# Weight preparation of an attention and SiLU network block on one NeuronCore: raw buffers, engine split and the order of the first loads

## The chip, the cores and the metric

The kernel runs on one core of a Trainium2 chip. The metric is device time in microseconds (us) of one execution. Five engines run side by side, each through its own instruction queue in order: TensorE (PE, matrix products and transposes; PEld is its weight load), VectorE (DVE), ScalarE (ACT), GpSimd (POOL) and SyncE (SP, which here only issues DMAs). Instructions wait for one another through semaphores.

## The reference

Eight batches of 576 tokens, eight heads of 64. Attention keeps only scores within `tau` of the row's maximum; its output, 4608 tokens of 512 features, goes through a two-layer network with 2048 hidden units.

```python
scores = scale * np.matmul(q, k.transpose(0, 1, 3, 2))
thresh = np.max(scores, axis=-1, keepdims=True) - tau
scores = np.where(scores >= thresh, scores, -1000000000.0)
scores = scores - np.max(scores, axis=-1, keepdims=True)
attn = np.exp(scores)
attn = attn / (np.sum(attn, axis=-1, keepdims=True) + 1e-09)
attn_out = np.matmul(attn, v)
...
h = x @ w_in
g = h * (1.0 / (1.0 + np.exp(-h)))
return g @ w_out
```

q, k and v are float32; w_in and w_out are float64 and reach the kernel as their raw words, so it decodes them itself.

## The kernel before, in words

**Tiles of attention.** The rows of the score matrices are cut into tiles of 128 query rows by 576 keys, one after the other. Batch 0 has 16 "low" tiles (tokens 0 to 255 of all heads; here called tiles 0 to 15), then 20 "high" ones (tiles 16 to 35); batch 1 has 16 and 20 as well (36 to 71); each later batch has 36. A tile passes through PE scores (`scores`, L452 in batch 0 in full float32, L464 later with split operands), DVE row maximum (L474), ACT exponential (L484), DVE mask and row sum (L493, with the small L477, L497 and L501), a scaling by the reciprocal row sum (POOL L507 in batch 0, ACT L511 later), and a transpose: in batch 0 on PE (L403, L408) with ACT copies out of PSUM (L416, L417), later by POOL splits into two float16 parts (L519, L522, L525) and a DMA transpose. Then `av_direct` (L426) or `av` (L550) multiplies by v, and `av_post` (L568, L569) writes the features x as two float16 parts. Only one PSUM bank holds an `a` product.

**The network.** For each half of a batch there are 16 h-units (L593: 12 products each, then ACT tanh L601, DVE L602, ACT L608, DVE L609, which leave the hidden layer in `gbuf` as two float16 parts) and 16 o-units (L624: 12 products each, four to an output block, ACT copy L634, store). The f-th h-unit needs four of the 16 blocks of w_in; every o-unit needs four blocks of w_out.

**The weights.** Each matrix is 16 blocks of 128 x 512. `load_weights` (L180) brings 512 KB of raw words to a buffer: half of the w_in blocks go to places in `gbuf` that the hidden layer doesn't use yet, the other half of w_in and all of w_out to a pool `wraw` with two buffers. `decode_weights` turns the words into float32 (ACT L190, DVE L193 and L196) and adds the block's Gram product to a PSUM bank (PE L208), from whose maximum (L213) `pow2_scales` forms one power-of-two scale for the matrix (L110 to L150). `split_weights` makes two float16 parts of each block: w_in by POOL (L225, scaling in place), ACT (L228) and POOL (L229, subtraction), w_out by ACT (L220) and DVE (L221).

**What sets the order.** The program is recorded in steps of one tile; `at(t, f)` puts work at step t, `W_PLAN` spreads loads, decodes, scale and splits of the two matrices over steps, and `pri` raises the priority of what it wraps. A scheduler then orders each engine's queue by priority and by a timeline that it keeps; on the chip the queues run in that order. `load_v` and `vmax` of batch 0 are at steps -4 and 0, where `vscale` follows at step 1.

Of the kernel before, what the change touches and what calls it, by code (L numbers as in the profile page):

```python
# [15 lines left out]
ALU = mybir.AluOpType  # L16
AX = mybir.AxisListType
# [18 lines left out]

W_PLAN = ((0, 0, 10, 13, 0), (16, 9, 22, 36, 0))
PRI_S, PRI_SOFT1, PRI_SOFT2 = 1600, 50, 200
# [13 lines left out]
def attention_moe(  # L52
# [52 lines left out]
    def pow2_scales(mx, name, own=None, squared=False):  # L105
# [6 lines left out]
        nc.scalar.activation(diag, ident, AF.Copy, scale=one)  # L112
        allp = bank([P, P], f"{name}_ps", own)
        nc.tensor.matmul(allp, ones, diag, start=True, stop=True)
# [53 lines left out]
    def load_weights(i):  # L168
        if i < 4 * NK and i % 8 < 4:
            o = 1024 * (i % 8)  # L170
            t = gbuf.bitcast(I32)[:, o : o + 1024].rearrange("p (c w) -> p c w", w=2)
        else:
            t = stage.tile([P, 512, 2], I32, tag="wraw", name=f"wraw_{i}", bufs=2)
        if i < 4 * NK:
            n, c = divmod(i, NK)
            src = w_words[0][c * P : (c + 1) * P, 1024 * n : 1024 * (n + 1)]
        else:
            f = i - 4 * NK
            src = w_words[1][f * P : (f + 1) * P, :]
        nc.sync.dma_start(out=t.rearrange("p c w -> p (c w)"), in_=src)  # L180
        wraw[i] = t

    def decode_weights(i):


        t = wraw.pop(i)
        low, top = t[:, :, 0], t[:, :, 1]
        w = wst[:, i + WSPARE, :]
        wbits = w.bitcast(I32)
        nc.scalar.activation(  # L190
            w, top.bitcast(F32), AF.Prelu, scale=2.0**-112, alpha=2.0**32
        )
        nc.vector.tensor_scalar(  # L193
            out=wbits, in0=wbits, scalar1=3, scalar2=None, op0=ALU.logical_shift_left
        )
        nc.vector.scalar_tensor_tensor(  # L196
            out=wbits, in0=low, scalar=29, in1=wbits,
            op0=ALU.logical_shift_right, op1=ALU.bitwise_or,
        )


        n, c = divmod(i, 4)
        if c == 0:
            wps[n] = bank([P, P], f"wps_{n}", 2)
        upper = w.bitcast(BF16).rearrange("p (c t) -> p c t", t=2)[:, :, 1]
        for j in range(4):
            part = upper[:, j * P : (j + 1) * P]
            nc.tensor.matmul(  # L208
                wps[n], part, part,
                start=(c == 0 and j == 0), stop=(c == 3 and j == 3),  # L210
            )
        if c == 3:
            nc.vector.tensor_reduce(out=wmx[:, n : n + 1], in_=wps[n], op=ALU.max, axis=AX.X)  # L213

    def split_weights(i):
        w = wst[:, i + WSPARE, :]
        hi = w16[:, i, 0:512]
        sc = wsc["in" if i < 4 * NK else "out"][:, 0:1]
        if i >= 4 * NK:
            nc.scalar.activation(hi, w, AF.Copy, scale=sc)  # L220
# [3 lines left out]
            return  # L224
        nc.gpsimd.tensor_scalar(  # L225
            out=w, in0=w, scalar1=sc, scalar2=1.0, op0=ALU.mult, op1=ALU.mult
        )
        nc.scalar.activation(hi, w, AF.Copy)  # L228
# [488 lines left out]
    for b in range(B):  # L717
        u = start[b, 0]
        for p in range(NPAIR):
            if b == 0:  # L720
                at(-4, lambda p=p: load_v(0, p))
                at(0, lambda p=p: vmax(0, p))
            elif b == 1:
# [3 lines left out]
            else:  # L727
# [3 lines left out]
                at(u + pace * p + pace // 2, lambda b=b, p=p: split_v(b, p))  # L731
        at((1, u + 2)[b] if b < 2 else u - 2, lambda b=b: vscale(b))

# [15 lines left out]
    for first, t0, t1, t2, hp in W_PLAN:  # L749
# [5 lines left out]
        for i in range(16):  # L755
            at(t1 + i * (t2 - t1) // 16, pri(hp, lambda i=i + first: split_weights(i)))
    at(W_PLAN[0][3], lambda: batch_scales_in(0))
# [23 lines left out]

    scores(0)
    t = 0
# [93 lines left out]
```

## Time and profile before

| what | value |
|---|---|
| median of 3 runs | 1230.53 us (1227.3 to 1231.17) |
| profiled execution | 1225.66 us, of which the span of its instructions is 1223.9 us |
| busy: PE, DVE, ACT, POOL | 1150.3, 933.7, 796.4, 707.5 us |
| granted PE clock, mean | 0.987 |
| chain that ended last | PE 63%, DVE 11%, DMA 10%, POOL 7% of the span |

The profile is of one execution. "Busy" is the time in which an engine has an instruction in work; for PE the ends are modelled. Idle time of an engine is given with what released the next instruction. "x40" is a count of instructions, and a float32 product counts as two.

### The profile page before, as it was taken

How to read it: one execution, taken by the hardware profiler on the slowest of the kernel's cores; microseconds unless marked ns; L12 is line 12 of the kernel's file. 1: busy time of each engine (PE TensorE's matmuls, PEld its weight loads, DVE VectorE, ACT ScalarE, POOL GpSimd, SP SyncE). 2: the span in 40 equal slices, each digit the busy share in tenths (PEclk: the TensorE clock that was granted, in tenths of full speed). 3: DMA queues.
4: the chain of work that ended last, by engine and by line, in shares of the span. 5: the costliest groups of instructions: out<-in, count | busy, mean ns of one | idle time of the engine just before them, and what ended most of it. 6: DMA issues, size and time to landing. Idle time of an engine off the chain costs nothing.

```text
span 1223.9 us, 27062 instructions
## 1 busy us (share of the span) xinstructions
PE 1150.3 (94%) x9474; PEld 899.2 (73%) x9474; DVE 933.7 (76%) x2625; ACT 796.4 (65%) x1505; POOL 707.5 (58%) x902
## 2 busy tenths in 40 slices
PE   6868799999899799999999999999999999999998
PEld 4545567777786577787777777788778877777777
DVE  7988988988999988889889858886788858333330
ACT  6667875876867777777777747785677756333331
POOL 2385357887877587886888428781778547100000
PEclk9979999999999999999999999999999999999999
DMA  9553148889788777886987448772877356200000
GB/s 309 185 161 95 41 108 173 160 160 177 132 177 141 160 137 139 150 165 151 167 149 145 114 94 155 146 136 82 153 150 142 77 92 116 42 11 16 16 10 25
DMA packets 340887, 151.73 MB, mean 124 GB/s; under 512 B 305936, under 2 KB 317200, under 8 KB 340752
## 3 DMA queue, kind: packets, MB, share of 16 engines
q1 hardware_dynamic: 340752, 150.01, 59.1%
q8 instruction: 75, 1.23, 0.4%
q14 instruction: 60, 0.49, 0.1%
HBM read 66.19 MB, written 9.44 MB: 62 GB/s over the span
## 4 chain that ended last, share of the span: by engine, by line
PE 63%; DVE 11%; DMA 10%; POOL 7%; issue 4%; ACT 4%; SPq 1%; POOLq 0%; ACTq 0%; DVEq 0%
PE o L624 24%; PE h L593 21%; PE s L464 9%; PE a L550 7%; DMA wT<-hl 4%; POOL hl L522 3%; DMA wraw<-in_w_out 3%; DVE w L493 2%; POOL hl L519 2%; DVE sm L474 2%; DVE qstack L350 2%; POOL hl L525 1%; DMA wraw<-in_w_in 1%; ACT w L484 1%; ACT w L511 1%
## 5 line engine op out<-in xcount | busy, mean ns | idle before, releaser
L593 PE MATMUL h<-x,wst 128*128 128x288 f16 (+2 forms) x3072 | 425.8, 288 | 7.8 <-DVE gbuf L609 5.0
L624 PE MATMUL o<-gbuf,wst 128*128 128x288 f16 (+2 forms) x3072 | 417.9, 286 | 2.4 <-ACT wst L634 2.4
L593 PEld LDWEIGHTS <-wst 128*128 128x128 f16 x3072 | 292.2, 98 | 95.7 <-issue 16.9
L624 PEld LDWEIGHTS <-wst 128*128 128x128 f16 x3072 | 292.7, 98 | 83.7 <-issue 7.4
L522 POOL TENSOR_TENSOR hl<-w,hl 128x512 f16<-128x512 f32 x252 | 302.6, 1201 | 12.8
L519 POOL TENSOR_SCALAR hl<-w 128x576 f16<-128x576 f32 x252 | 172.2, 686 | 193.4 <-ACT w L511 115.7
L484 ACT ACTIVATE w<-s,sm 128x576 f32<-128x576 f32 x288 | 211.6, 739 | 91.9 <-DVE sm L474 39.1
L493 DVE SCALAR_TENSOR_TENSOR w<-s,sm,w 128x576 f32<-128x576 f32 x288 | 232.0, 812 | 39.9 <-ACT w L484 37.8
L474 DVE TENSOR_REDUCE sm<-s 128x1 f32<-128x576 f32 x288 | 214.4, 749 | 28.7 <-PE s L464 21.8
L511 ACT ACTIVATE w<-w,sm 128x576 f32<-128x576 f32 x252 | 191.4, 771 | 52.1 <-DVE sm L501 50.1
L602 DVE SCALAR_TENSOR_TENSOR h<-th,h 128x288 f32<-128x288 f32 (+2 forms) x256 | 116.2, 455 | 113.7 <-ACT th L601 112.3
L601 ACT ACTIVATE th<-h,msc 128x288 f32<-128x288 f32 (+2 forms) x256 | 126.6, 498 | 103.2 <-PE h L593 101.8
L464 PE MATMUL s<-khi,qstack 128*128 128x288 f32 x560 | 144.3, 338 | 12.7 <-DVE w L493 9.9
L608 ACT ACTIVATE gbuf<-h 128x288 f16<-128x288 f32 (+2 forms) x256 | 104.3, 408 | 78.2 <-DVE h L602 77.5
L609 DVE SCALAR_TENSOR_TENSOR gbuf<-h,gbuf 128x288 f16<-128x288 f32 (+2 forms) x256 | 115.3, 452 | 41.9 <-ACT gbuf L608 41.0
L550 PE MATMUL a<-wT,v 128*64 128x288 f16 (+2 forms) x1568 | 115.0, 289 | 10.8 <-DMA wT<-hl 10.6
L360 POOL TENSOR_TENSOR klo<-kraw,khi 128x576 fp32r<-128x576 f32 x64 | 94.5, 1476 | 47.1 <-ACT khi L358 47.0
L464 PE MATMUL s<-klo,qstack 128*128 128x288 f32 x560 | 120.8, 296 | 0.0
L464 PEld LDWEIGHTS s<-khi,qstack 128*128 128x128 f32 x560 | 87.7, 190 | 31.9 <-issue 15.4
L550 PEld LDWEIGHTS <-v 128*64 128x64 f16 x1568 | 84.5, 110 | 33.7 <-issue 22.1
L464 PEld LDWEIGHTS s<-klo,qstack 128*128 128x128 f32 x560 | 90.4, 189 | 0.6
L525 POOL TENSOR_TENSOR hl<-w,hl 128x64 f16<-128x64 f32 x252 | 89.5, 355 | 0.0
(101 smaller groups left out, 930.4 us busy)
## 6 DMA issues: line engine op xcount, KB each, us to landing
kraw<-in_kT SPq DMA_DIRECT2D x128, 144.0 KB, 3.0
qraw<-in_qT SPq DMA_DIRECT2D x96, 144.0 KB, 3.0
vraw<-in_vL SPq DMA_DIRECT2D x32, 320.0 KB, 3.6
wraw<-in_w_out SPq DMA_DIRECT2D x16, 512.0 KB, 3.7
out_t<-wst SPq DMA_DIRECT2D x48, 144.0 KB, 2.1
wT<-hl SPq DMA_TRANSPOSE x280, 3.4
gbuf<-in_w_in SPq DMA_DIRECT2D x8, 512.0 KB, 6.2
wraw<-in_w_in SPq DMA_DIRECT2D x8, 512.0 KB, 5.1
```

What stands on the lines that cost most here:

```text
L464: nc.tensor.matmul(s_ps[:, j, :HALF], lhs, kk[:, j * HALF : (j + 1) * HALF], start=(n == 0), stop=(n == len(seq) - 1),)
L474: nc.vector.tensor_reduce(out=negm, in_=s_ps[:, :, :HALF], op=ALU.max, axis=AX.XY, negate=True)
L484: nc.scalar.activation(wtile[t].rearrange("p (j c) -> p j c", j=2), sps[t][:, :, :HALF], AF.Exp, bias=small[t][:, 0:1],)
L493: nc.vector.scalar_tensor_tensor(out=w3, in0=s_ps[:, :, :HALF], scalar=sm[:, 1:2], in1=w3, op0=ALU.is_ge, op1=ALU.mult, accum_out=sm[:, 2:3],)
L511: nc.scalar.activation(w, w, AF.Copy, scale=r)
L519: nc.gpsimd.tensor_scalar(out=fl[:, 0:S], in0=w, scalar1=1.0, scalar2=1.0, op0=ALU.mult, op1=ALU.mult)
L522: nc.gpsimd.tensor_tensor(out=fl[:, 640:1152], in0=w[:, 0:512], in1=fl[:, 0:512], op=ALU.subtract)
L550: nc.tensor.matmul(a_ps[odd * D : (odd + 1) * D, :n], vt[:, lo_v, odd, kv, :], wT[v, b * H + 2 * p + odd][:, kw, c0 - base : c0 - base + n ...
L593: nc.tensor.matmul(ph[:, :n], wi(c, f, lo_w), x16[b, lo_x][:, c, c0 : c0 + n], start=(k == 0), stop=(k == 11),)
L601: nc.scalar.activation(th[:, :n], ph[:, :n], AF.Tanh, scale=moe_sc[b][:, 0:1])
L602: nc.vector.scalar_tensor_tensor(out=ph[:, :n], in0=th[:, :n], scalar=1.0, in1=ph[:, :n], op0=ALU.add, op1=ALU.mult,)
L624: nc.tensor.matmul(ps[:, :n], wo(f, d, lo_w), g[:, lo_g, :n], start=(f == 0 and k == 0), stop=(f == NF - 1 and k == 2),)
```

## The change

Five things change.

- The raw-word buffers: besides the w_in blocks that already lie in `gbuf`, every block whose number leaves 2 or 3 when divided by 4 now goes to one of two further places there (6400 and 7424), so `wraw` with its two buffers holds only the other blocks.
- The second parts: odd blocks of w_in are split by ACT and one DVE instruction, even ones stay with POOL, ACT, POOL. Blocks of w_out are scaled in place by a DVE instruction (new), copied by ACT, and subtracted by POOL.
- Loads, decodes and scale of w_out get priority 150; no split gets a raised one. The splits of w_out are spread to step 38, from 36.
- v of batch 0 is loaded at step -1, its maximum is at step 2 and its scale at step 3. The first `scores` gets a raised priority.
- The product with which the scale of w_out is spread over partitions writes into the second half of the last Gram bank, instead of a bank taken anew.

```diff
-W_PLAN = ((0, 0, 10, 13, 0), (16, 9, 22, 36, 0))
+W_PLAN = ((0, 0, 10, 13, 0), (16, 9, 22, 38, 150))
...
-        allp = bank([P, P], f"{name}_ps", own)
+        allp = wps[7][:, P : 2 * P] if name == "o_w" else bank([P, P], f"{name}_ps", own)
...
     def load_weights(i):
         if i < 4 * NK and i % 8 < 4:
             o = 1024 * (i % 8)
+        else:
+            o = (None, None, 6400, 7424)[i % 4]
+        if o is not None:
             t = gbuf.bitcast(I32)[:, o : o + 1024].rearrange("p (c w) -> p c w", w=2)
         else:
             t = stage.tile([P, 512, 2], I32, tag="wraw", name=f"wraw_{i}", bufs=2)
...
     def split_weights(i):
-        if i >= 4 * NK:
+        if i < 4 * NK and i % 2:
             nc.scalar.activation(hi, w, AF.Copy, scale=sc)
             nc.vector.scalar_tensor_tensor(
                 out=w16[:, i, 512:1024], in0=w, scalar=sc, in1=hi, op0=ALU.mult, op1=ALU.subtract
             )
             return
-        nc.gpsimd.tensor_scalar(
-            out=w, in0=w, scalar1=sc, scalar2=1.0, op0=ALU.mult, op1=ALU.mult
-        )
+        if i < 4 * NK:
+            nc.gpsimd.tensor_scalar(
+                out=w, in0=w, scalar1=sc, scalar2=1.0, op0=ALU.mult, op1=ALU.mult
+            )
+        else:
+            nc.vector.tensor_scalar(out=w, in0=w, scalar1=sc, scalar2=None, op0=ALU.mult)
         nc.scalar.activation(hi, w, AF.Copy)
         nc.gpsimd.tensor_tensor(
             out=w16[:, i, 512:1024], in0=w, in1=hi, op=ALU.subtract
...
-                at(-4, lambda p=p: load_v(0, p))
-                at(0, lambda p=p: vmax(0, p))
+                at(-1, lambda p=p: load_v(0, p))
+                at(2, lambda p=p: vmax(0, p))
...
-            at(t1 + i * (t2 - t1) // 16, pri(hp, lambda i=i + first: split_weights(i)))
+            at(t1 + i * (t2 - t1) // 16, pri(0, lambda i=i + first: split_weights(i)))
...
-    scores(0)
+    pri(2 * PRI_S, lambda: scores(0))()
```

The scheduler's order moves with it, on all engines, over the first half of the program. Three places follow. The first is the start of DVE's queue, `sm` being a tile's small column, `s` its scores, `w_0` its exponentials, `wst` the decoded weights, `v`-names the scale of v. Before:

```order
L390 TENSOR_SCALAR gbuf<-gbuf,gate 64x256 x2
L474 TENSOR_REDUCE sm_132<-s_129 128x1
L474 TENSOR_REDUCE sm_183<-s_136 128x1
L477 TENSOR_SCALAR sm_132<-sm_132,ntau 128x1
L268 TENSOR_REDUCE vmx_161<-vps_140 128x1
L477 TENSOR_SCALAR sm_183<-sm_183,ntau 128x1
L493 SCALAR_TENSOR_TENSOR w_0_133,sm_132<-s_129,sm_132,w_0_133 128x576
L110 TENSOR_REDUCE v_one<-vmx_161 128x1
L193 TENSOR_SCALAR wst<-wst 128x512
```

And in the changed kernel (its lines are 6 higher from there on, L196 is the old L193 and L199 the old L196):

```order
L396 TENSOR_SCALAR gbuf<-gbuf,gate 64x256 x2
L480 TENSOR_REDUCE sm_132<-s_129 128x1
L196 TENSOR_SCALAR wst<-wst 128x512
L483 TENSOR_SCALAR sm_132<-sm_132,ntau 128x1
L199 SCALAR_TENSOR_TENSOR wst<-gbuf,wst 128x512
L499 SCALAR_TENSOR_TENSOR w_0_133,sm_132<-s_129,sm_132,w_0_133 128x576
L480 TENSOR_REDUCE sm_160<-s_136 128x1
```

The first decode moved ahead of the first mask, and the maximum of v far back.

The second is POOL's queue where the splits of w_in begin; `w_13` and so on are exponentials that wait for their scaling. Before:

```order
L507 TENSOR_SCALAR w_13_754<-w_13_754,sm_753 128x576
L225 TENSOR_SCALAR wst<-wst,i_w_sc 128x512 x16
L229 TENSOR_TENSOR wst<-wst 128x512 x2
L507 TENSOR_SCALAR w_14_795<-w_14_795,sm_794 128x576
L507 TENSOR_SCALAR w_15_839<-w_15_839,sm_838 128x576
L507 TENSOR_SCALAR w_28_1137<-w_28_1137,sm_1136 128x576
```

And now:

```order
L513 TENSOR_SCALAR w_14_779<-w_14_779,sm_778 128x576
L229 TENSOR_SCALAR wst<-wst,i_w_sc 128x512 x8
L235 TENSOR_TENSOR wst<-wst 128x512 x2
L513 TENSOR_SCALAR w_15_823<-w_15_823,sm_822 128x576
L513 TENSOR_SCALAR w_28_1120<-w_28_1120,sm_1119 128x576
L235 TENSOR_TENSOR wst<-wst 128x512 x2
```

The block of scalings between two tiles is half as long, and stands one tile later.

The third is PE's queue where the first o-unit (`o_0_0`) begins; `a_3_256` is the last product of batch 0 with v, `s` with `khi` a score of batch 1, `h_0_15` the last h-unit of the first half. Before:

```order
L426 MATMUL a_3_256_2038<-wT_6_1787,vraw_3_117 64x320
L426 MATMUL a_3_256_2038<-wT_7_1880,vraw_3_117 64x320
L464 MATMUL s_2151<-khi_2013,qstack_85 128x288 x2
L464 MATMUL s_2151<-klo_2015,qstack_85 128x288 x2
L624 LDWEIGHTS wst
L624 MATMUL o_0_0_1535<-gbuf,wst 128x256
```

And now:

```order
L599 MATMUL h_0_15_1490<-x_0_1_443,wst 128x256
L599 LDWEIGHTS wst
L599 MATMUL h_0_15_1490<-x_0_0_442,wst 128x256
L630 LDWEIGHTS wst
L630 MATMUL o_0_0_1529<-gbuf,wst 128x256
```

Before, the o-units begin behind the scores of tile 41 and the end of batch 0's attention; now they begin behind the scores of tile 33, with tiles 34 and 35 of batch 0 still to come.

More of the change, by code (lines that the diff above doesn't have):

```diff
@@ L203, in decode_weights @@
         if c == 0:
-            wps[n] = bank([P, P], f"wps_{n}", 2)
+            wps[n] = bank([P, 2 * P if n == 7 else P], f"wps_{n}", 2)
         upper = w.bitcast(BF16).rearrange("p (c t) -> p c t", t=2)[:, :, 1]
@@ L208, in decode_weights @@
             nc.tensor.matmul(
-                wps[n], part, part,
+                wps[n][:, 0:P], part, part,
                 start=(c == 0 and j == 0), stop=(c == 3 and j == 3),
@@ L212, in decode_weights @@
         if c == 3:
-            nc.vector.tensor_reduce(out=wmx[:, n : n + 1], in_=wps[n], op=ALU.max, axis=AX.X)
+            nc.vector.tensor_reduce(out=wmx[:, n : n + 1], in_=wps[n][:, 0:P], op=ALU.max, axis=AX.X)
     def split_weights(i):
@@ L731, in attention_moe @@
                 at(u + pace * p + pace // 2, lambda b=b, p=p: split_v(b, p))
-        at((1, u + 2)[b] if b < 2 else u - 2, lambda b=b: vscale(b))
+        at((3, u + 2)[b] if b < 2 else u - 2, lambda b=b: vscale(b))
     def pri(offset, f):
```

## The prediction

> **What bounds the kernel now.** I read the busy times by stretch first, then groups by line, then the timeline at the ends of stages.
>
> ```profile
> core 0: us, PE busy (x) PEld busy (x) DVE busy (x) ACT busy (x) POOL busy (x), PEclk, DMA share, GB/s
> 0.00:60.00 60.00, 45.66 (x282) 30.25 (x283) 50.64 (x163) 38.03 (x74) 15.31 (x28) 0.97 0.76 247
> 60.00:75.40 15.40, 8.76 (x42) 4.59 (x40) 12.41 (x33) 9.12 (x18) 15.38 (x19) 0.92 0.52 157
> 75.40:111.00 35.60, 27.11 (x152) 18.30 (x153) 30.05 (x68) 26.56 (x55) 26.89 (x25) 0.80 0.48 150
> 111.00:178.00 67.00, 57.51 (x385) 40.81 (x385) 57.58 (x170) 49.73 (x111) 23.05 (x25) 0.95 0.20 52
> 178.00:210.30 32.30, 31.16 (x292) 26.83 (x291) 27.36 (x65) 19.29 (x35) 24.56 (x28) 1.00 0.82 185
> 210.30:253.70 43.40, 39.19 (x325) 29.48 (x324) 41.52 (x120) 37.26 (x72) 36.60 (x46) 1.00 0.83 157
> 253.70:450.00 196.30, 179.70 (x1518) 141.28 (x1516) 177.15 (x492) 142.85 (x257) 151.99 (x195) 0.99 0.81 156
> 450.00:1050.00 600.00, 590.66 (x5089) 471.82 (x5086) 489.76 (x1416) 419.60 (x768) 413.75 (x539) 1.00 0.70 133
> ```
>
> From 450 us on PE is busy 98% of the time: nothing there is to be had. PE's idle time lies ahead: 29.5 us to 111, 9.5 to 178, 1.1, 4.2, then 16.6 to 450. To 111 us DVE has most work (93.1 us); 60 to 75.4 belongs to POOL.
>
> The stages end with the last maximum of a w_out block (A, 111), the last product for the first 16 h-units' results (B, 178), 16 o-units (C, 210.3, where PE's next h-unit starts) and 16 more h-units (D, 253.7):
>
> ```profile
> 110.82 0.27 DVE L213 TENSOR_REDUCE wmx<-wps 128x1 f32<-128x128 f32 x1
> 177.42 0.41 DVE L609 SCALAR_TENSOR_TENSOR gbuf<-h,gbuf 128x256 f16<-128x256 f32 x1
> 210.09 0.57 PE L593 MATMUL h<-x,wst 128*128 128x320 f16 x3
> 251.73 1.93 PE L593 MATMUL h<-x,wst 128*128 128x320 f16 x13
> ```
>
> **Stage A: what goes and what comes.** The start, and the POOL block:
>
> ```profile
> 2.87 2.01 SPq L250 DMA_DIRECT2D vraw<-in_vL  x4
> 8.73 1.42 DVE L474 TENSOR_REDUCE sm<-s 128x1 f32<-128x576 f32 x2 [3.15 <-PE s L452]
> 11.12 0.66 ACT L190 ACTIVATE wst<-gbuf 128x512 f32<-128x512 f32 x1 [0.85 <-DMA gbuf<-in_w_in]
> 60.02 12.72 POOL L225 TENSOR_SCALAR wst<-wst,i_w_sc 128x512 f32<-128x512 f32 x16 [2.51 <-DVE i_w_sc L145]
> 75.39 3.67 POOL L507 TENSOR_SCALAR w<-w,sm 128x576 f32<-128x576 f32 x4
> ```
>
> Before, tile 0's second score product stands behind tile 1's, and the four loads of v ahead of w_in. Undone, the first maximum comes one tile's two products sooner, 3.15 of idle shrinking by some 1.8 us (between 0 and 3.15). The four v loads, passed on SP's queue by two w_in blocks, then delay blocks 2 and 3 instead; v itself is not needed before tile 1 is transposed. Net: 1.8. From 60 to 75.4 no L507 runs, so no tile is transposed; now eight scalings and two subtractions stand there.
>
> ```profile
> L193 DVE TENSOR_SCALAR wst<-wst x32: 404/426/1281, 11.8 to 108.1; 128x512 int32<-128x512 int32 x32
> L196 DVE SCALAR_TENSOR_TENSOR wst<-wraw,wst 128x512 int32<-128x512 int32 x24 | 20.2, 842 | 0.1
> L196 DVE SCALAR_TENSOR_TENSOR wst<-gbuf,wst 128x512 int32<-128x512 int32 x8 | 5.4, 680 | 0.0
> L193 DVE TENSOR_SCALAR wst<-wst 128x512 int32<-128x512 int32 x32 | 17.8, 557 | 7.5 <-ACT wst L190 7.5
> L190 ACT ACTIVATE wst<-wraw 128x512 f32<-128x512 f32 x15 | 10.1, 675 | 12.0 <-DMA wraw<-in_w_out 12.0
> L493 DVE SCALAR_TENSOR_TENSOR w<-s,sm,w 128x576 f32<-128x576 f32 x25 | 20.0, 807 | 1.5 <-ACT w L484 1.3
> L474 DVE TENSOR_REDUCE sm<-s 128x1 f32<-128x576 f32 x26 | 19.2, 746 | 4.0 <-PE s L452 4.0
> L477 DVE TENSOR_SCALAR sm<-sm,ntau 128x1 f32<-128x1 f32 x26 | 5.2, 203 | 0.1
> L501 DVE RECIPROCAL sm<-sm 128x1 f32<-128x1 f32 x24 | 3.7, 153 | 0.1
> L221 DVE SCALAR_TENSOR_TENSOR wst<-wst,o_w_sc x16: 726/743/1485, 124.6 to 150.3; 128x512 f16<-128x512 f32 x16
> L229 POOL TENSOR_TENSOR wst<-wst x16: 1147/1326/1611, 72.7 to 105.2; 128x512 f16<-128x512 f32 x16
> ```
>
> ACT waited 12.0 us for w_out's raw blocks, which wait for two buffers; that made 7.5 us of idle on DVE. With four buffers I take half of it away. In the changed program, seven tiles fewer stand on DVE ahead of the last decode (19 maxima for 26, 17 masks for 24), because w_out's decode has priority: 7 x (0.746 + 0.807 + 0.203 + 2 x 0.153) = 14.4 us; with one x part and two h parts gone (some 1.3 us) and two L221 kinds come (1.5), 14.2. L193 and L196 took 17.8 - 32 x 0.426 = 4.2 and 20.2 - 24 x 0.68 = 3.9 us over their undisturbed times, nearly all while POOL worked; POOL's work on w_in now lies later and is half, so I take 4 off. A: 93.1 - 14.2 - 4 = 75 busy, and of 17.9 idle 1.8 and 3.75 go: **87 us** instead of 111 (76 with no idle but the start's and no disturbance, 97 with all of both).
>
> **Stage B.** Counted in the order, DVE loses against before: ten L221 kinds (7.4), two masks, two splits of q, a v maximum, one scale, about 5 us; and gets 16 scalings of w_out. No row shows float32 scaling on DVE at this size; L193 has its shape with one input: 0.43 to 1.28. I take 0.43: 6.9. So 57.6 - 12.4 + 6.9 = 52. On PE:
>
> ```profile
> L452 PE MATMUL s<-kd,gbuf 128*128 128x288 f32 x40 | 11.9, 423 | 2.7 <-DVE w L493 2.7
> L403 PE MATMUL tm<-ident,w 128*128 128x128 f32 x52 | 8.4, 286 | 3.8 <-ACT wT L416 3.7
> L408 PE MATMUL tl<-ident,w 128*128 128x128 f32 x13 | 3.8, 289 | 0.9 <-ACT wT L417 0.9
> L593 PE MATMUL h<-x,wst 128*128 128x256 f16 x168 | 22.8, 291 | 2.5 <-DVE gbuf L609 2.5
> L464 PE MATMUL s<-khi,qstack 128*128 128x288 f32 x20 | 5.1, 337 | 0.7 <-DVE w L493 0.7
> L464 PE MATMUL s<-klo,qstack 128*128 128x288 f32 x20 | 4.3, 294 | 0.0
> L550 PE MATMUL a<-wT,v 128*64 128x256 f16 x56 | 3.7, 275 | 0.4 <-DMA wT<-hl 0.4
> ```
>
> A tile of batch 0 costs 1.19 us of scores (four rows of 40) and 0.94 of transposes, one of batch 1 0.94 of scores (ten tiles). B now holds all 16 h-units (2 more, 3.3 us) and 15 scores of batch 0 instead of 10 with 4 of batch 1 (2.2): 63 us. Before, 9.5 were idle; with DVE lighter I take 6: **69** (63 to 73). POOL's 16 subtractions of w_out (16 x 1.33 = 21 us) lie beside this: it was busy 23 of 67. B ends at 156, not 178: 22 us ahead.
>
> But less is done there: six tiles' scores (6.2), seven tiles' transposes (6.6), half an `a` pair (1.6) are owed on PE, 14.4 us; on DVE about 21 (seven maxima, nine masks and what goes with them). So 22 us of lead are **7.6** if PE bounds what follows, 1 if DVE does.
>
> **C and D.** C keeps its o-units, swaps 11 scores of batch 1 (10.3), two `a` products (56 rows, 3.7) and part of an h-unit (1.2) for 6 scores (6.2) and 7 transposes (6.2, some rows run ahead): 3 us less on PE, 29. It ends at 185 instead of 210.3; PE now owes 17.4. DVE has only six tiles there instead of 11, and owes 21 + 5 x 2.06 = 31. D gets five tiles more: DVE 41.5 + 5 x 2.06 + some 2 of splits = 54, above PE's 48; with 1.9 idle as before, 56. D ends at 241, 12.7 ahead, and PE owes six scores and one `a` product, 5.6 + 1.9 = 7.5: a gain of 5. By the 64th h-unit, near 430, it owes five scores and two products, 8.4. **Gain: about 4.** Further on both orders come together, on a stretch where PE is never idle for long, so I let the 4 stand.
>
> The sum is against the profiled execution: 1223.9 - 4 = 1219.9 of span, with 1.8 around it 1221.7 where it had 1225.66. That one is 4.9 below the median; on the median of 1230.53 it is 1226.5.
>
> **Edits at nothing.** ACT swaps eight L220 for eight L228 of about the same length, beside PE's bound in B. The new places in `gbuf` are read out by the decode in A, long before the hidden layer's second half gets there in D; were they not, its h parts would wait. The scale's product in the last Gram bank saves a wait for a bank that the h-units use, and is at most one unit, 22.8 / 14 = 1.6 us, inside B's 63 to 73. A later end of w_out's splits (step 38) is covered by the h-units in front of the first o-unit; bare, it would cost one POOL subtraction, 1.3 us.
>
> [...] The mean L193 is 0.56 us with a longest of 1.28, so POOL does cost DVE time. [...]
>
> **The rivals.**
>
> *The scalings wait (slower).* The 16 scalings of w_out stand nearly in one burst on DVE, between the second and third h-unit's parts. Masks and h parts are queued behind them, the two h banks are full, and PE waits. At the longest L193, 1.28, they take 20.5 instead of 6.9, 13.6 more: 1226.5 + 13.6 = 1240. From 0.43 + 4/16 = 0.68 each on the gain is gone. For it: the disturbed L193; against: half of them ran at 0.426. Chance 0.12.
>
> *What is owed is paid on DVE (slower).* In C DVE is idle half the time. If the stages to 450, where it was busy 90%, must make up all of the 31 us, the lead of 25 is spent and 6 more: 1236. It decides from D at 60 us on, where the lead (253.7 - 185 - 60 = 8.7) is about what PE owes. For it: the row to 450; against: PE has 16.6 us idle there too. Chance 0.13.
>
> [...] If the tiles' pipeline no longer stops, A ends at 80 and B holds 66: 10 more, 1216. For it: PE's granted clock of 0.80 behind the stop; against: DVE is 84% busy. Chance 0.20.
>
> *No gain.* If buffers weren't it, DMAs being late for another cause, A takes 91 and the 4 are gone: 1230.5. Chance 0.10.
>
> **How the numbers follow.** The forecast has 0.45, spread from 1222 to 1230. About 0.3% (3.7 us) is what a measurement can tell from none; half the forecast's chance (0.22) is beyond it. Faster: 0.22 + 0.20 = 0.42. Same: 0.23 + 0.10 + 0.02 of the slower cases = 0.35. Slower: 0.23. Range: 1215, just under the faster rival, to 1237; beyond it lie most of the first rival and the far ends of A.
>
> **What would show it.** The first maximum near 7 us; no wait of 12 us for w_out's raw blocks; last L213 at 87; last h part of the first half at 156; o-units done near 185; then DVE above 95% busy to 241, and the idle of PE to 450 below 61 by about 4. A mean of the new scaling above 0.68 us, or PE idle above 20 us from 241 to 450, would make it wrong.

## The result, and the profile after

| | before | changed kernel |
|---|---|---|
| median of 4 runs each | 1229.93 us (1227.3 to 1231.17) | 1239.11 us (1236.54 to 1241.56) |
| profiled execution, its span | 1225.66, 1223.9 us | 1241.56, 1239.8 us |
| PE busy, granted clock | 1150.3 us, 0.987 | 1159.2 us, 0.981 |

The ratio is 1.0075, with an interval of 1.0051 to 1.0098: 9 us slower, where 4 us faster was forecast, and 2 us above the upper end of the range. The change does what it says: v is loaded later, the first maximum begins at 7.10 us, ACT waits 4.5 us for w_out's raw blocks instead of 12, and the decode ends 25 us sooner. All of that is spent again, and more.

These are the busy times by stretch of the changed kernel, cut at the ends of its own stages A (85.5), B (157.1), C (190) and D (257.1). The columns are the length, busy time and count for each engine, then the granted PE clock, the DMA share and GB/s.

```profile
0.00:60.00 60.00, 45.23 (x261) 29.92 (x262) 51.21 (x157) 39.26 (x75) 12.88 (x25) 0.94 0.87 299
60.00:85.50 25.50, 18.30 (x110) 12.04 (x110) 23.78 (x64) 17.42 (x34) 16.50 (x17) 0.87 0.45 148
85.50:157.10 71.60, 58.80 (x377) 42.22 (x374) 55.52 (x157) 48.02 (x108) 40.48 (x39) 0.90 0.11 30
157.10:190.00 32.90, 32.71 (x269) 26.98 (x268) 16.69 (x47) 15.34 (x35) 8.20 (x10) 1.00 0.29 63
190.00:257.10 67.10, 52.99 (x408) 37.83 (x406) 62.61 (x165) 50.85 (x97) 48.79 (x61) 0.92 0.74 156
257.10:450.00 192.90, 175.77 (x1445) 137.09 (x1444) 168.03 (x475) 137.76 (x245) 148.25 (x187) 0.97 0.78 152
450.00:1050.00 600.00, 588.93 (x5071) 469.82 (x5069) 504.15 (x1447) 430.23 (x781) 426.67 (x555) 1.00 0.70 136
```

A, B and C end where the prediction had them, within 5 us (B here at the end of PE's last h product; the last h part, which the prediction marks, begins at 159.36). D is 67.1 us long instead of 56, and PE stands idle for 14.1 us of it. But B is not as sound as its end: PE is idle for 12.8 us in it, and the clock of 0.90 is the lowest but for 60 to 85.5.

**The stop in B.** This is the timeline of VectorE in the changed kernel where the scale of w_out comes: start, length, engine, line, operation and count. L233 is the new scaling of a w_out block.

```profile
102.56 0.14 DVE L145 TENSOR_SCALAR o_w_sc<-o_w_e 128x1 f32<-128x1 f32 x1
...
103.08 2.96 DVE L233 TENSOR_SCALAR wst<-wst,o_w_sc 128x512 f32<-128x512 f32 x5
105.96 0.80 DVE L499 SCALAR_TENSOR_TENSOR w<-s,sm,w 128x576 f32<-128x576 f32 x1
...
106.77 6.12 DVE L233 TENSOR_SCALAR wst<-wst,o_w_sc 128x512 f32<-128x512 f32 x7
112.81 0.42 DVE L608 SCALAR_TENSOR_TENSOR h<-th,h 128x256 f32<-128x256 f32 x1
113.14 0.87 DVE L233 TENSOR_SCALAR wst<-wst,o_w_sc 128x512 f32<-128x512 f32 x2
...
114.60 1.47 DVE L233 TENSOR_SCALAR wst<-wst,o_w_sc 128x512 f32<-128x512 f32 x2
...
116.06 0.41 DVE L608 SCALAR_TENSOR_TENSOR h<-th,h 128x256 f32<-128x256 f32 x1
...
117.05 0.41 DVE L615 SCALAR_TENSOR_TENSOR gbuf<-h,gbuf 128x256 f16<-128x256 f32 x1
```

And this is PE's timeline there:

```profile
108.00 0.66 PE L409 MATMUL tm<-ident,w 128*128 128x128 f32 x4
108.49 0.27 PE L414 MATMUL tl<-ident,w 128*128 128x128 f32 x1
117.51 5.28 PE L599 MATMUL h<-x,wst 128*128 128x256 f16 x24 [8.74 <-DVE gbuf L615]
```

When the scale exists, all 16 blocks are ready at once, and the queue holds the 16 scalings nearly side by side: 2.96 + 6.12 + 0.87 + 1.47 = 11.4 us. From the first of them to 113.9 one mask (L499) and one h part (L608) get through, besides two instructions on a single column. PE cannot start the next h-unit before the parts of an earlier one have left its bank, and stands for 8.74 us. In the page of the changed kernel the same wait shows as the idle time before h-units as a whole, 18.0 us where the page of before has 7.8, 14.1 of it ended by L615:

```profile
L599 PE MATMUL h<-x,wst 128*128 128x288 f16 (+2 forms) x3072 | 429.7, 288 | 18.0 <-DVE gbuf L615 14.1
```

**The bill behind a stop.** Busy times of the changed kernel in the stop and in the two stretches behind it:

```profile
108.80:117.50 8.70, 0.00 (x0) 0.00 (x0) 8.70 (x16) 4.34 (x10) 5.34 (x6) 0.74 0.00 0
117.50:123.10 5.60, 5.59 (x26) 3.91 (x26) 3.31 (x14) 3.94 (x8) 5.60 (x7) 0.50 0.00 1
123.10:130.00 6.90, 6.90 (x49) 5.54 (x49) 5.30 (x16) 5.63 (x13) 5.93 (x7) 1.00 0.19 55
```

For 5.6 us behind the stop PE is busy at a granted clock of 0.50: it does 26 products there, and 49 in the next 6.9 us. Products of one shape (L599, 128x256) start 0.213 us apart in the first stretch and 0.109 apart in the second. So this stop cost its length and some more. This gives a better measure of progress than stage ends. Over a whole run the span is PE's work at full clock, plus PE's idle time, plus half of the time that PE works at 0.50. I summed the last two over the trace up to PE's last product, and call them **lost time**. Before lost 70.3 + 12.7 = 83.0 us of its span of 1223.9, and the changed kernel 77.3 + 18.5 = 95.8 of 1239.8; 3.3 us follow PE's last product in both. The work at full clock is what remains, 1137.6 and 1140.7. So of 15.9 us of span 12.8 are lost time: 7.0 idle, 5.8 clock. What is lost up to a point is also comparable in the middle of two runs whose stages hold different work:

| us lost up to | 85 | 160 | 200 | 260 | 450 | 600 | the end |
|---|---|---|---|---|---|---|---|
| before | 30 | 46 | 50 | 55 | 74 | 75 | 83 |
| changed kernel | 28 | 45 | 46 | 63 | 85 | 89 | 96 |

At the end of B the changed kernel had its 16 h-units 16 us sooner (PE's last product for them ends at 157.1 instead of 173.0), and was ahead by **1 us** at most: the rest was work of tiles not yet done. From 200 to 260 it loses 17 us where before lost 5.

Two limits of the measure. The trace's first clock record stands at 8.1 us before and at 13.9 in the changed kernel, and what lies ahead of it counts as full clock. The products there are slow, though: in both kernels those of the first scores start 0.48 us apart ahead of the first record, and 0.24 behind it. Counted as half clock, that adds 1.5 us to before, 4.4 to the changed kernel, 4.5 to act_scales below and 1.5 to 2.9 to every other run, in each column. The changed kernel's lead of 1 us at 160 is then 2 us behind, and lost time makes 15.7 of the 15.9 us. These 2.9 us between the two runs seem to be the draw of one execution: after_late_order, whose order is the same to about 410 us, has its first record at 8.2. And the work at full clock that remains is not the same in all runs (1132 to 1137 us, so counted), so the measure leaves up to 5 us of a difference unexplained.

**D.** VectorE's timeline in the changed kernel, where batch 1's v gets its scale and is split (L318), and the maxima of batch 2's v (L278) follow:

```profile
198.37 0.14 DVE L145 TENSOR_SCALAR v_sc<-v_e 128x1 f32<-128x1 f32 x1
...
199.02 1.15 DVE L308 SCALAR_TENSOR_TENSOR msc<-msc,o_w_sc 128x1 f32<-128x1 f32 x1
200.10 1.01 DVE L318 SCALAR_TENSOR_TENSOR v<-vraw,v_sc,v 128x640 f16<-128x640 f32 x1
...
201.70 1.86 DVE L318 SCALAR_TENSOR_TENSOR v<-vraw,v_sc,v 128x640 f16<-128x640 f32 x1
...
204.27 1.71 DVE L318 SCALAR_TENSOR_TENSOR v<-vraw,v_sc,v 128x640 f16<-128x640 f32 x1
205.90 0.81 DVE L278 TENSOR_REDUCE vmx<-vraw 128x1 f32<-128x640 f32 x1
206.63 0.87 DVE L318 SCALAR_TENSOR_TENSOR v<-vraw,v_sc,v 128x640 f16<-128x640 f32 x1
...
207.54 0.54 DVE L575 SCALAR_TENSOR_TENSOR x<-a,xscale,x 128x320 f16<-128x320 f32 x1
```

PE's waits from 190 to 257, summed by line and releaser (total, times, longest):

```profile
PE a L556 <- DVE x L575: 4.9, 1, 4.9
PE s L470 <- DVE w L499: 4.6, 2, 3.2
PE h L599 <- ACT x L574: 2.3, 1, 2.3
```

It is the same picture: the splits of v become ready together with their scale, and stand ahead of L575, for which PE's only `a` bank waits. D is also long because more is in it: scores of 19 tiles, where before has 14.5 in its D.

### The profile page after: what moved, and what is told of

Read it like the earlier page. It is cut to its first block, busy times and chain, and to the rows that moved or that the text cites. A ratio compares the mean times of both kernels' runs of the same rounds, so it can differ in the third digit from the quotient of the medians.

```text
span 1239.8 us, 27045 instructions
## 1 busy us (share of the span) xinstructions
PE 1159.2 (93%) x9474; PEld 904.5 (73%) x9474; DVE 937.3 (76%) x2633; ACT 800.6 (65%) x1505; POOL 710.1 (57%) x902
## 4 chain that ended last, share of the span: by engine, by line
PE 57%; DVE 21%; DMA 7%; ACT 5%; issue 5%; POOL 4%; SPq 0%; POOLq 0%; DVEq 0%; ACTq 0%
PE h L599 20%; PE o L630 20%; PE s L470 7%; PE a L556 6%; DVE w L499 5%; DMA wT<-hl 4%; DVE sm L480 4%; DVE qstack L356 3%; PE s L458 2%; ACT w L517 2%; DMA vraw<-in_vL 2%; ACT w L490 2%; DVE h L608 2%; PE a L432 2%; POOL hl L528 1%
## 5 line engine op out<-in xcount | busy, mean ns | idle before, releaser
L599 PE MATMUL h<-x,wst 128*128 128x288 f16 (+2 forms) x3072 | 429.7, 288 | 18.0 <-DVE gbuf L615 14.1
L599 PEld LDWEIGHTS <-wst 128*128 128x128 f16 x3072 | 292.3, 98 | 108.3 <-issue 28.2
L528 POOL TENSOR_TENSOR hl<-w,hl 128x512 f16<-128x512 f32 x252 | 303.3, 1204 | 13.6
L499 DVE SCALAR_TENSOR_TENSOR w<-s,sm,w 128x576 f32<-128x576 f32 x288 | 232.6, 812 | 46.8 <-ACT w L490 44.6
L608 DVE SCALAR_TENSOR_TENSOR h<-th,h 128x288 f32<-128x288 f32 (+2 forms) x256 | 116.6, 456 | 107.1 <-ACT th L607 105.0
L470 PE MATMUL s<-khi,qstack 128*128 128x288 f32 x560 | 144.3, 339 | 17.5 <-DVE w L499 13.6
L615 DVE SCALAR_TENSOR_TENSOR gbuf<-h,gbuf 128x288 f16<-128x288 f32 (+2 forms) x256 | 115.4, 452 | 41.6 <-ACT gbuf L614 40.7
L556 PE MATMUL a<-wT,v 128*64 128x288 f16 (+2 forms) x1568 | 120.9, 296 | 15.8 <-DMA wT<-hl 10.7
L556 PEld LDWEIGHTS <-v 128*64 128x64 f16 x1568 | 87.0, 112 | 41.2 <-issue 25.4
```

The costliest lines, as they stand in the source:

```text
L470: nc.tensor.matmul(s_ps[:, j, :HALF], lhs, kk[:, j * HALF : (j + 1) * HALF], start=(n == 0), stop=(n == len(seq) - 1),)
L499: nc.vector.scalar_tensor_tensor(out=w3, in0=s_ps[:, :, :HALF], scalar=sm[:, 1:2], in1=w3, op0=ALU.is_ge, op1=ALU.mult, accum_out=sm[:, 2:3],)
L528: nc.gpsimd.tensor_tensor(out=fl[:, 640:1152], in0=w[:, 0:512], in1=fl[:, 0:512], op=ALU.subtract)
L556: nc.tensor.matmul(a_ps[odd * D : (odd + 1) * D, :n], vt[:, lo_v, odd, kv, :], wT[v, b * H + 2 * p + odd][:, kw, c0 - base : c0 - base + n ...
L599: nc.tensor.matmul(ph[:, :n], wi(c, f, lo_w), x16[b, lo_x][:, c, c0 : c0 + n], start=(k == 0), stop=(k == 11),)
L608: nc.vector.scalar_tensor_tensor(out=ph[:, :n], in0=th[:, :n], scalar=1.0, in1=ph[:, :n], op0=ALU.add, op1=ALU.mult,)
```

## Experiments

Each kernel was timed beside the kernel before on the same chip. "Lost" is the measure above; a stop is a wait of PE.

| kernel | ratio, interval | lost to 160 | 260 | 450 | 600 | end |
|---|---|---|---|---|---|---|
| before | 1 | 46 | 55 | 74 | 75 | 83 |
| the changed kernel | 1.0075, 1.0051 to 1.0098 | 45 | 63 | 85 | 89 | 96 |
| act_scales | 1.0095, 1.006 to 1.013 | 45 | 56 | 77 | 88 | 97 |
| wo_split_as_before | 1.0007, 0.9984 to 1.003 | 41 | 51 | 67 | 81 | 89 |
| scalings_tied | 1.0017, 0.9997 to 1.0036 | 42 | 56 | 78 | 79 | 90 |
| only_wo_split | 1.0121, 1.01 to 1.0143 | 52 | 62 | 80 | 88 | 99 |
| wo_split_tied_alone | 1.0066, 1.0042 to 1.0091 | 43 | 56 | 79 | 85 | 97 |
| v_early | 1.0076, 1.0052 to 1.01 | 51 | 62 | 77 | 86 | 94 |
| act_v_early | 0.9988, 0.9971 to 1.0006 | 47 | 56 | 74 | 78 | 87 |
| tied_v_early | 0.9938, 0.9911 to 0.9965 | 38 | 45 | 64 | 67 | 75 |
| wo_old_v_early | 0.999, 0.997 to 1.0009 | 41 | 47 | 68 | 74 | 86 |
| only_buffers | 1.0049, 1.0032 to 1.0066 | 51 | 61 | 79 | 87 | 96 |
| only_v_first_scores | 1.0069, 1.0052 to 1.0086 | 47 | 58 | 78 | 83 | 95 |
| only_w_in_half | 1.001, 0.9994 to 1.0026 | 46 | 61 | 77 | 84 | 90 |
| order_only | 1.0172, 1.0151 to 1.0193 | 52 | 68 | 85 | 99 | 111 |
| before_late_order | 0.9987, 0.9971 to 1.0004 | 44 | 53 | 73 | 75 | 82 |
| after_late_order | 1.0094, 1.0067 to 1.0122 | 50 | 67 | 89 | 93 | 100 |
| tied_late_order | 1.0018, 1.0001 to 1.0034 | 39 | 54 | 80 | 81 | 90 |
| wo_old_late_order | 1.0004, 0.9988 to 1.002 | 41 | 52 | 69 | 85 | 92 |
| tied_v_late_order | 0.9915, 0.9889 to 0.9942 | 41 | 47 | 67 | 71 | 79 |

**Is it the burst?** The expectations number their theories anew in each batch, and say what each is. act_scales has the 16 scalings on ACT:

```diff
-            nc.vector.tensor_scalar(out=w, in0=w, scalar1=sc, scalar2=None, op0=ALU.mult)
+            nc.scalar.activation(w, w, AF.Copy, scale=sc)
```

> The changed kernel with one edit: the 16 in-place scalings of w_out run on ScalarE instead of VectorE. Theory 1 (the burst of 16 scalings, 103 to 116 us, stands in front of the h-units' second parts, and TensorE's wait of 8.7 us there is lost for good): that wait falls below 2 us, 16 o-units are done near 183 instead of 190, and the ratio to the kernel before falls from 1.0075 to about 1.001 to 1.003. Theory 2 (what counts is VectorE work owed at the end of the o-units, paid in the stage behind): the o-units are done earlier, but the next 16 h-units end within 3 us of 257 and the ratio stays above 1.005.

wo_split_as_before has no scalings; w_out is split by ACT and one VectorE instruction, as before, and the rest of the change stays:

```diff
-        if i < 4 * NK and i % 2:
+        if i >= 4 * NK or i % 2:
```

> The changed kernel with w_out's blocks split as before (ScalarE and one VectorE instruction each, no scaling, no GpSimd subtraction). Theory 1: no burst, the wait of 8.7 us falls below 2 us; VectorE has 16 x 0.74 us of second parts instead of 16 x 0.48 us of scalings, spread between tiles; ratio 1.000 to 1.004. Theory 2: the second stage still waits for VectorE, 16 h-units end near 257, ratio above 1.005.

scalings_tied has the same 16 scalings, but records them with the VectorE part of h-units 4 to 15 (f) of the first half, and makes each depend on that h-unit's tanh by a one-column instruction that copies the scale. The copies on ACT and the subtractions on POOL move with them:

```diff
+                nc.vector.scalar_tensor_tensor(
+                    out=sc, in0=th[:, 0:1], scalar=0.0, in1=wsc["out"][:, 0:1],
+                    op0=ALU.mult, op1=ALU.add,
+                )
+                for j in (2 * f - 8, 2 * f - 7) if f < 8 else (f,):
+                    split_weights(4 * NK + j, sc)
```

> The changed kernel, with the same 16 scalings of w_out on VectorE, but each waits (through a column of its own, formed from an h-unit's tanh) for one of the h-units 4 to 15, so that they can't stand in one burst. 16 tiny VectorE instructions more. Theory 1 (the burst's place in VectorE's queue, not its work, stops TensorE): the wait of 8.7 us at 108.8 us falls below 2 us, the 16 h-units are done near 151 instead of 157, and as with w_out's old split the ratio comes to 1.000 to 1.003. Theory 3 (early stalls hardly matter; each order loses or gains some us between 300 and 750 us, and the scalings on ScalarE already removed part of the wait and gained nothing): the wait goes, but the ratio stays at 1.005 or more.

`only_wo_split` puts the new split of w_out, and nothing else of the change, into the kernel before; `wo_split_tied_alone` is that with the scalings tied in the same way.

> The kernel before with only the new split of w_out (scaling on VectorE, copy on ScalarE, subtraction on GpSimd). Theory 1: the scalings stand in one burst here too, ratio 1.003 to 1.008. A rival, that the burst costs only because w_out is decoded early and the h-units are waiting for it: the burst falls where tiles are short of nothing, ratio within 0.002 of 1.

> The kernel before with nothing but w_out's new split, and with each scaling tied to one h-unit, so that no burst can form (as only_wo_split, 1.0121, without its burst; twelve tiny VectorE instructions are added). If the burst costs the time: PE's stop of 7.9 us near 130 goes, and the ratio falls by 0.006 or more, to 1.000 to 1.006. If the split itself costs it, or only the order that came out by chance: the ratio stays above 1.008.

On ACT the scalings are still one burst. These are the durations (min/median/max ns, first and last start) of L233 in act_scales:

```profile
L233 ACT ACTIVATE wst<-wst,o_w_sc x16: 775/792/807, 102.9 to 115.1; 128x512 f32<-128x512 f32 x16
```

and PE's longest wait from 85 to 160 in the same kernel has only changed its name, to transposes that wait for ACT's copies:

```profile
PE tl L414 <- ACT wT L423: 5.5, 1, 5.5
```

Tied to twelve h-units, the same 16 scalings cost no stop above 2.3 us. PE's largest waits in scalings_tied there:

```profile
PE h L599 <- DVE gbuf L615: 3.5, 2, 2.3
PE tl L414 <- ACT wT L423: 1.8, 1, 1.8
```

though the middle one takes as long as before, 0.48 us (all 16 together take 9.2 instead of 11.4 us); L233 in scalings_tied, and in the changed kernel:

```profile
L233 DVE TENSOR_SCALAR wst<-wst,tied x16: 470/484/1286, 111.7 to 153.3; 128x512 f32<-128x512 f32 x16
```

```profile
L233 DVE TENSOR_SCALAR wst<-wst,o_w_sc x16: 473/480/1380, 103.1 to 115.6; 128x512 f32<-128x512 f32 x16
```

The same holds in the kernel before. There the burst stops the scores; PE's largest wait from 85 to 160 in only_wo_split is

```profile
PE s L455 <- DVE w L496: 9.7, 5, 7.9
```

and tied, in wo_split_tied_alone, it is

```profile
PE s L455 <- DVE w L496: 4.5, 7, 1.2
```

PE's first wait above that comes behind this window, at 166.7: 3.3 us, for ACT's copies. So the stop of 7.9 us is the burst's, like that of 8.7: it comes with it in two programs and on two engines, and goes with it in both programs. Without it the ratio falls from 1.0075 to 1.0017, and from 1.0121 to 1.0066. In the first pair the lost time up to 260 falls by 7 us (10 with the start counted), in the second by 6. What wo_split_tied_alone still loses lies behind 260: 56 there against 55 before, and 97 against 83 at the end.

Not all of the expectations were met. act_scales missed its first theory (a stop of 5.5 us, not below 2, and 1.0095), and its second in that the next 16 h-units ended at 246 and not near 257. It lost 7 us less than the changed kernel up to 260, and 11 from 450 to 600: the ratio doesn't follow from the early stops alone. only_wo_split came out above its 1.003 to 1.008, and wo_split_tied_alone fell by 0.0055 where 0.006 was asked for.

**Is it the v of batch 1?** Here its four raw blocks get a place of their own in `gbuf`, and loads, maxima, scale and splits come some steps earlier, into C, where the changed kernel's VectorE is busy 16.7 of 32.9 us.

```diff
+        if b == 1:
+            o = 6400 + 640 * p
+            t = gbuf.bitcast(F32)[:, o : o + 640].rearrange("p (a k d) -> p a k d", a=2, k=5)
...
-                at(u + 5 * p - 20, lambda p=p: load_v(1, p))
+                at(u + 2 * p - 16, lambda p=p: load_v(1, p))
...
-                at(u + (4 if 1 in HALVED else 9) * p + 4, lambda p=p: split_v(1, p))
+                at(u + p - 4, lambda p=p: split_v(1, p))
...
-        at((3, u + 2)[b] if b < 2 else u - 2, lambda b=b: vscale(b))
+        at((3, u - 5)[b] if b < 2 else u - 2, lambda b=b: vscale(b))
```

> The changed kernel with v of batch 1 loaded into places of gbuf that are free between w_out's decode and the second half of the hidden layer, and its maximum, scale and split recorded some 6 steps earlier, so that VectorE does them while TensorE is on the o-units. Theory 2 (VectorE's four splits and the scale of v, 199 to 207 us, stand in front of the second part of the last attention product of batch 0, and TensorE waits 4.9 and 3.2 us): the next 16 h-units end near 249 instead of 257 and the ratio falls to about 1.001. Theory 1 (the burst alone): the 8.7 us wait stays, the stage behind the o-units stays at 65 us or more, ratio within 0.002 of 1.0075.

> Both edits together. If the two waits are separate and each is lost for good: the gains add, ratio 0.993 to 0.998. If VectorE's sum of work sets the end of the next 16 h-units, whatever its order: no better than the better one of the two alone by more than 0.002.

> The tied scalings with the early v of batch 1. Theory 1 and 2 together (each of the two stops alone is made up for by the other, both gone is a gain): ratio 0.994 to 0.999, as with scalings on ScalarE and early v. Theory 3: anything from 0.998 to 1.008, not ordered by TensorE's idle time before 260 us.

> The changed kernel with w_out's old split and the early v of batch 1: both stops removed in the cheapest way. If they add: 0.994 to 0.998. If the early v does nothing without the burst: within 0.002 of 1.0007.

D does shrink: from the end of w_out's 16 o-units on it takes 54.6 us in v_early (192.6 to 247.2) instead of 67. That does not show what v costs, since less is in it: scores of 15.5 tiles instead of 19. And D is as short where v stays as it was and only w_out's scalings change: 56.8 us in act_scales, 55.7 in wo_split_as_before and 57.5 in scalings_tied, with 15 to 16 tiles in it, although PE still waits 3.7 us for L575 in scalings_tied. By lost time from 200 to 260 the changed kernel's 17 us become 10 in v_early and 5 to 9 in these three. With the burst in place the end is where it was, 1.0076: v_early lost 6 us more than the changed kernel up to 160 (3 with the start counted). With the scalings tied the whole change comes to **0.9938**, faster than both kernels, with 45 us lost up to 260. PE's waits from 160 to 260 in tied_v_early no longer name L575:

```profile
PE a L560 <- DMA wT<-hl: 2.8, 2, 2.1
PE h L603 <- DVE gbuf L619: 2.5, 2, 1.5
PE s L474 <- DVE w L503: 1.0, 1, 1.0
```

Two things do not fit a simple sum. With w_out's old split the earlier v brings almost nothing (1.0007 to 0.999, the second of its expectations), and with the scalings on ACT it brings 0.011 (0.9988, between its two expectations).

**The parts alone**, each put into the kernel before: the raw buffers (`o = (None, None, 6400, 7424)[i % 4]`), v of batch 0 behind the first blocks of w_in together with the first scores' priority, and the odd blocks of w_in on ACT and VectorE (`if i >= 4 * NK or i % 2:`).

> The kernel before with nothing but the two more raw buffers (blocks with i % 4 of 2 and 3 beyond the first half of w_in are loaded into columns 6400 and 7424 of gbuf). Theory 1 (the buffers bring the early decode, and that lead is no gain, since the work of the tiles that it passes is owed and paid later): the last Gram product of w_out ends near 90 us instead of 110.5, the first half's h-units near 155 to 165 instead of 173, and the lead is gone by h-unit 128 near 720; ratio 0.997 to 1.003. Theory 2 (the early decode is itself the harm, since the tiles fall behind): ratio above 1.005.

> The kernel before with nothing but v of batch 0 loaded behind the first blocks of w_in and the first tile's scores with priority. Theory 1: the first maximum comes near 7 us, some 2 us sooner, and nothing else lasts: ratio 0.996 to 1.002, no stop of PE above 4 us in 85 to 160. Theory 2 (the later v is what makes the changed kernel slower): ratio above 1.005.

> The kernel before with nothing but the second parts of w_in's odd blocks made on ACT and VectorE instead of on GpSimd (GpSimd's scaling and subtraction of eight blocks go, eight activations and eight VectorE instructions of 0.7 us come). Theory 1: POOL is busy some 15 us less before 110, DVE some 6 us more; the splits of w_in are off the path as h-units wait for w_out's decode anyway: ratio 0.997 to 1.004. Theory 2 (the 6 us more on DVE, which is busy 84% there, go straight into the span): ratio 1.004 to 1.006.

The half of w_in costs nothing, as expected. The buffers alone cost 0.5%, just between their two theories, and the later v 0.7%, as its second theory had it, neither with a burst of scalings. With the buffers the last Gram product ends at 82.5 us instead of 110.5, and 51 us are lost by 160 against 46: the decode's lead is here a loss. The four parts sum to 2.5%, and together they cost 0.75%. So they are not terms of a sum. The other edits (w_out's priority of 150, its splits up to step 38, the scale's product in the last Gram bank) were not run alone. The losses of the buffers and of the later v lie in many small stops, and I did not find one cause for them; whether the order that they bring about decides is not shown.

**How much is mere order?** `order_only` is the changed kernel with another priority for the splits of w_out, and nothing else.

```diff
-            at(t1 + i * (t2 - t1) // 16, pri(0, lambda i=i + first: split_weights(i)))
+            at(t1 + i * (t2 - t1) // 16, pri(-200 if first else 0, lambda i=i + first: split_weights(i)))
```

> A control: the changed kernel with a priority lower by 200 for the splits of w_out. The burst of 16 scalings stays where it was on DVE, between the second and the third h-unit, and nothing is added or taken away; some tiles and v splits change places by a few positions behind it. If the burst is what costs the time: PE's stop of 7 to 9 us near 110 stays and the ratio to before is 1.005 to 1.010. If the differences between the runs are only a matter of the order in which the scheduler happens to put the rest: the stop stays, and the ratio is anywhere, 0.998 to 1.004 as likely as not.

The burst and its stop stayed, and the ratio rose to 1.0172, outside both expectations. It lost 6 us more than the changed kernel up to 160 (4 with the start counted), and 14 from 450 to 600, where the changed kernel lost 4. So a shuffle alone can move this kernel by 1%, as much as the effects in question. The controls that follow shuffle only what comes behind 410 us, in five kernels:

```diff
-                at(u + pace * p - first + 6, lambda b=b, p=p: vmax(b, p))
+                at(u + pace * p - first + 8, lambda b=b, p=p: vmax(b, p))
```

> A control: the kernel before with the maxima of v of batches 2 and later two steps later. The order is the same to about 410 us and shuffled by some positions after that; nothing is added or taken away. If the late order alone can move the time: the idle and half-clock time of PE from 450 to 600 (1 us before, 1 to 14 in the runs so far) differs by several us, and the ratio by as much, between 0.997 and 1.011. If it can't: 0.998 to 1.002.

> The same control on the changed kernel: order the same to about 410 us, shuffled after. What was lost up to 260 (burst and batch 1's v) stays, 63 us of idle and half-clock time against 55 before. If that loss is what makes the changed kernel slower: 1.004 to 1.012. If its slowness came from the late order: below 1.004.

> The same control on the changed kernel with the scalings tied (1.0017). Its 56 us of idle and half-clock time up to 260 stay. If the loss up to 260 decides: 0.998 to 1.006, that is 0.003 or more below after_late_order; if the late order decides, the two can stand either way.

> The order control (maxima of v of batches 2 and later two steps later, order the same to about 410 us) on wo_split_as_before, which stood 7 us ahead of before in idle and half-clock time at 450 us (67 against 74) and lost 14 from 450 to 600 (before 1). If that loss was an accident of the late order: 1 to 5 us from 450 to 600 here, and a ratio of 0.990 to 0.997. If the lead is a debt that is called in there in any order: 10 us or more again, and 0.999 to 1.004.

> The same control on tied_v_early, the fastest so far (0.9938). If its gain is made before 410 us (45 us of idle and half-clock time at 260, before 55): the ratio stays between 0.990 and 0.998. If it was a lucky late order: above 0.998.

All five stayed within 0.25% of the kernels that they shuffle: 0.9987, 1.0094, 1.0018, 1.0004 and 0.9915. The changed kernel's loss, the gain of tying and the gain of tied_v_early all survive. The shuffle is a mild one, though. In wo_split_as_before 14 us are lost from 450 to 600, the largest piece in these PE waits of that kernel:

```profile
PE s L470 <- DVE w L499: 7.3, 4, 4.5
PE a L556 <- DMA wT<-hl: 2.5, 2, 1.4
```

and the shuffled wo_old_late_order has both rows again with the same numbers, so the control did not touch that place. Whether the 7 us that this kernel is ahead at 450 are lost there by a debt or by an accident of the order stays open, and so do the 14 us of order_only.

## Why the prediction was wrong, step by step

- **A, 87 us: right.** The last maximum of w_out's blocks starts at 85.59. VectorE was busy 51.21 + 23.78 = 75.0 us, as worked out, the first maximum came at 7.10, and ACT's wait for w_out's raw blocks fell from 12.0 to 4.5 (for w_in's it rose from 2.8 to 5.6).
- **B, 156 us: near, by two errors.** The mark, the last h part, came at 159.4, 3 us late; PE's last h product ended at 157.1. PE needed less than the 63 us that were reckoned (58.8 busy, at a clock of 0.90), and lost more: 12.8 idle for 6.
- **"I take 0.43: 6.9": the size was off, and its place was not counted.** An undisturbed scaling takes 0.48 us, and the first four start 0.40 apart, so 0.43 was fair for those. But seven of the 16 began while an instruction of POOL was running, and took 0.56 to 1.38 us; the other nine, beside two of which POOL began later, took 0.47 to 0.48. The mean was 0.77, past the 0.68 that the first rival gave as its mark, and the row took 11.4 us instead of 6.9. The longest, of 1.38 us, began 0.30 us after a subtraction of POOL (L235) that took 1.40; by what means POOL slows VectorE no run shows. The disturbance made the row longer; it does not by itself stop PE, since the tied scalings of wo_split_tied_alone take up to 1.51 us and PE has no wait above 1.2 us up to 160. The harm is that the 16 stand in a row: it costs a stop of 8.7 us and 5.6 us at half clock behind it. The first rival had named that mechanism; the forecast spread the 6.9 over B as busy time of an engine with slack. That the rival's 1240 is near the measured 1239.1 is luck: it priced 13.6 us of longer scalings, and 4.5 came.
- **"22 us of lead are 7.6": wrong.** What is owed was counted from the order, and PE's own losses were left out of that count. By lost time the lead at 160 was 1 us. With the burst away it was 4 to 5 (41 in wo_split_as_before and 42 in scalings_tied, against 46).
- **"with 1.9 idle as before, 56": the step that failed.** D took 67.1 us, and PE was busy for 53.0 of it (48 were reckoned) and idle for 14.1 (8 reckoned). What PE owed at its end was counted rightly, scores of 6.5 tiles and one `a` product for six and one. VectorE's 62.6 busy us exceed the reckoned 54: the "some 2 of splits" were 5.4 us of splits of v and 4.0 of maxima of batch 2's v. Their place was not counted either: 4.9 + 2.3 us are PE waiting for parts of x behind batch 1's v on VectorE and ACT, and 6.6 us of PE's work in D ran at half clock. The second rival's condition, D at 60 us or more, was met, and VectorE was busy 93% of D, as that rival has it. How much of the 11 us is v's stays open, as D is shorter without the burst too.
- **Where D came out as reckoned, there was no gain either.** In scalings_tied the last h product, the o-units and D end at 150, 184 and 241.4 (forecast 156, 185 and 241), and D, with scores of 15 tiles in it, has VectorE busy for 53.9 and PE for 48.3 us. But by then PE owes scores of 8.5 tiles and two `a` products, by the prediction's prices 8.0 + 3.7 us against a lead of 12.3, and the ratio is 1.0017.
- **"Gain: about 4": wrong by 17 us of lost time** (a gain of 4, a loss of 12.8). Of these 12.8, 8 are there at 260 (63 against 55; 11 more than before with the start counted), and 5 come later. Removing the burst takes back some 7 of the ratio's 9 us (1.0017 for 1.0075), and with it most of the 8.
- **"I let the 4 stand", since PE is never idle for long from 450 on: not safe.** It held for the changed kernel within 2 us from 600 on (7 against 8), but from 450 to 600 these kernels lost anything from 1 to 16 us.
- **Not in the sum at all: the clock.** 5.8 of the 12.8 us are work at half clock. The prediction gave the granted clock, 0.80 from 75.4 to 111 us, as support for its faster rival, not as a price.

What is shown: the burst makes the stop, and two ways of having none make the whole change cost nothing measurable (1.0017, 1.0007). Not shown: why buffers and later v lose when they are alone, and how much of each ratio is order. The sign is the same in every pair that differs in tying alone (0.6, 0.8, 0.6 and 1.4%: the changed kernel, its late_order, only_wo_split and v_early, each against its tied twin), though two of these pairs share their order up to 410 us. A size below 1% is not firm, since order_only moved as much.

## What to carry to other kernels

When a shared scale releases many equal instructions at once, don't price them as busy time: price the row that they make in an engine's queue, and what stands behind it; tying each to the unit of work that runs beside it cost here twelve tiny instructions and gave back 7 us. Compare two orders by idle time and half-clock time up to the same moment, not by the stage that is done: 16 us of lead were 1 at most. And before a difference below 1% of a scheduled kernel is given to a cause, run one kernel that changes nothing but the order.

## What the runs showed of the hardware

In two traces the granted clock fell on a grid. In before and in the changed kernel the periods at 0.50 begin whole multiples of 3.41 us apart and last 3.41 us or a multiple of it (up to 13.65), counted up to 1180 us. The phase of the grid is not the same: the first of them begin at 25.13 and at 37.83 us, 1.24 and 0.28 us past a multiple of 3.41 from the span's start. 14 of the 15 periods follow a grid window in which PE was busy 0.48 or less of the time (0.68 ahead of the other, at 37.83). Of the windows at full clock behind PE's first product that were busy 0.48 or less, one was not followed by such a period (0.44, from 417.67 in before). So a window that is half idle was nearly always enough here: the one from 404.01 in before, with a wait of 2.4 us for a DMA of which 2.0 lie in it and PE busy 0.41 of the time, is followed by 3.41 us at 0.50 in which PE is busy throughout. By that, a stop of 2 us inside one window can cost another 1.7 us (an estimate: half of 3.41, if PE is busy through the window behind it).

The new scaling, float32 in place at 128x512 on VectorE, takes 0.47 to 0.48 us in the nine of the changed kernel that began while POOL ran nothing, and ACT's takes 0.78 to 0.81 in act_scales (the middle one 0.79).
